# Agent attention with an ELU feed-forward on one core: how the two output accumulators are summed

## The chip, the cores and the metric

The kernel runs on one core of a Trainium2 chip. The metric is the device time of one execution in microseconds; the time before is 998.0 us, the median of three runs (997.5 to 999.86).

## The reference, cut to what matters

```python
def attn(q, k, v, agents):            # q, k, v: 2 x 12480 x 128; agents: 2 x 49 x 128, all fp32
    sm = lambda a, b: softmax(a @ b.T / sqrt(128))
    return sm(q, agents) @ (sm(agents, k) @ v)

def moe(x, w_in, w_out):              # x: 24960 x 128; w_in: 128 x 2048; w_out: 2048 x 128
    h = x @ w_in
    g = where(h > 0, h, exp(min(h, 0)) - 1)
    return g @ w_out                  # 24960 x 128, fp32
```

The product of the agents' values with `w_in` is formed once per batch (a 49 x 2048 matrix A), so that h is the softmax of q over the 49 agents times A.

## The kernel before, in words

**Tiles.** The 24960 tokens are 26 groups of 960, and a group is two halves of 480 columns (T). The 2048 rows of the hidden layer are 8 chunks (NP) of 256, held as two banks of 128 partitions. One **step** s handles one chunk of one half; there are 416 steps. Eight steps in a row (a **cycle**) share one pair of output accumulators, so there are 52 cycles.

**A step** (loop at L720) issues, in this order:
- `p1(s)` (L405): six matmuls on TensorE, in three pairs, write h into a slot of two PSUM banks. There are three slots (`ps_h`, bufs=3). The two matmuls of a pair use different rows of the array and run side by side.
- at the fifth step of each cycle, in a cycle without a "visit" in the step before, `p1(s + 1)` is issued too (L727).
- `p2(s - 4)` (L437): the matmuls with `w_out` add a chunk that is four steps old into the two accumulators: six pairs where g was split into a high and a low part, and otherwise two fp32 products, which the trace shows as four pairs.
- `elu(s)` (L416): ScalarE's Relu of h (L419) and Exp (L422), then VectorE's g (L424), which reads h from PSUM and ends the slot's use.
- `split(s)` (L427): for four or five of eight chunks VectorE casts g (L431), and GpSimd makes the low part in two subtractions (L204).
- extra work from two tables: `mid`, before `elu`, holds the normalisation of the next group's probabilities (`q_mul`, L325) or a subtraction (`e_sub`, L208), always at the fourth step of a cycle; `pre`, at the end of the step, holds score matmuls ("visits", which take an h slot), loads and the rest of the softmax.

There is no scheduler: each engine runs its own instructions in the order in which the loop writes them (`manual_schedule`). Waits come from the tiles: the first matmul into a tile waits until the last reader of the tile that had this place before is done.

**The accumulators** are `o0` and `o1`, one PSUM bank each, in the pool `ps_o` with bufs=1 (L65, L440). So the first `p2` of a cycle, which falls in the fifth step (s % 8 == 4), cannot write before those of the cycle before have been read; and that reading is issued at the end of `p2` in the fourth step (s % 8 == 3).

**The sum** of the two accumulators takes three engines (L454 to L472): VectorE copies `o1` to `ob` (L465, in `p2`); ScalarE copies `o0` to `oa` (L468, between Relu and Exp of the same step's `elu`, through the argument `between`); GpSimd adds `oa` to `ob` (L469); SyncE sends `ob` out (L470). This is done 51 times; the last cycle sums in two pieces on ScalarE and VectorE (L460 to L463).

**The visits** fall on the fourth step of 17 of these 51 cycles (`plan`, L659 to L669, with s % 8 == EDGE == 3). There the score matmuls and one `p1` lie between the last `p2` of a cycle and the first of the next. In the other 34, called quiet here, two `p1` lie there: twelve matmuls in six pairs.

The start-up (about the first 60 us) borrows `o0` and `o1` for scores of k (L537) and for parts of A (L608).

Of the kernel before, what the change touches and what calls it, by code (L numbers as in the profile page):

```python
# [8 lines left out]
F32 = mybir.dt.float32  # L9
# [3 lines left out]
ACTF = mybir.ActivationFunctionType  # L13
ALU = mybir.AluOpType
AX = mybir.AxisListType
# [9 lines left out]
def tile_agent_attention_moe(  # L25
# [10 lines left out]
    nc = tc.nc  # L36
# [7 lines left out]
    T = G // 2  # L44
    NG = N // G
    NR = NG
    S = B * NG * NM
# [17 lines left out]
    ps_o = ctx.enter_context(tc.tile_pool(name="ps_o", bufs=1, space=bass.MemoryType.PSUM))  # L65
# [3 lines left out]
    ident = const.tile([128, 128], F32)  # L69
# [3 lines left out]
    win_sb = big.tile([C, DFF], F32)  # L73
# [63 lines left out]
    def slot(dt=F32):  # L137

        return ps_h.tile([128, 2, 512], dt, tag="h", name="h")
# [9 lines left out]
    def attn_free(ps):  # L149
        if held.pop(id(ps), None) is not None:  # L150
            idle.append(ps)
# [3 lines left out]
    def scores_pe(ps, src, b, lo, hi):  # L155
        for j in range(lo, hi):
            for u in range(0, TP, groups[0]):
                w = min(groups[0], TP - u)
                x = j * TP + u
                nc.tensor.matmul(out=ps[u:u + w, j * NA:(j + 1) * NA], lhsT=src[:, x:x + w], rhs=ag_sb[:, b, :], start=True, stop=True)  # L160
# [3 lines left out]
    def k_copy(ps, r):  # L164
        nc.scalar.activation(out=s_all[:, r, 0:R, :].rearrange("p t a -> p (t a)"), in_=ps[:TP, 0:R * NA], func=ACTF.Copy)

    def k_red(view, r):
        nc.vector.tensor_reduce(out=m_all[:, :, r], in_=view.rearrange("p (t a) -> p a t", a=NA), axis=AX.X, op=ALU.max)  # L168
# [225 lines left out]
    h_t, e_t, g_t, hi_t, lo_t, o_t = {}, {}, {}, {}, {}, {}  # L394

    def at_step(s):

        x, c = divmod(s, NP)
        return x // 2, x % 2, c

    def is_split(s):
        j, half, c = at_step(s)
        return c in SPLITS[half if j * NM + NP + LAG in covered else 0]

    def p1(s):  # L405
        j, half, c = at_step(s)
        h = slot()
        ah, al = A[j // NG, c]
        hi, lo = p_t[j]
        for i, (a, p) in enumerate([(ah, hi), (ah, lo), (al, hi)]):  # L410
            for u, r in enumerate(ROWS):
                x = slice(r, r + NA)
                nc.tensor.matmul(out=h[:, u, 0:T], lhsT=a[x, :], rhs=p[u ^ half][x, :], start=i == 0, stop=i == 2)  # L413
        h_t[s] = h[:, :, 0:T]

    def elu(s, between=None):  # L416

        h, e = h_t.pop(s), x_p.tile([128, 2, T], F32, tag="e", name="e")
        nc.scalar.activation(out=e, in_=h, func=ACTF.Relu, scale=-1.0)  # L419
        if between:  # L420
            between()
        nc.scalar.activation(out=e, in_=e, func=ACTF.Exp, scale=-1.0)  # L422
        g = g_p.tile([128, 2, T], F32, tag="g", name="g", bufs=5)
        nc.vector.scalar_tensor_tensor(out=g, in0=e, scalar=-1.0, in1=h, op0=ALU.add, op1=ALU.max)  # L424
        g_t[s] = g
# [11 lines left out]
    def p2(s):  # L437
        j, half, c = at_step(s)
        if c == 0:
            o_t[0] = ps_o.tile([128, 512], F32, tag="o0", name="o0")  # L440
            o_t[1] = ps_o.tile([128, 512], F32, tag="o1", name="o1")
        g = g_t.pop(s)
        first, last = c == 0, c == NP - 1
        if is_split(s):
            x, hi, lo = SPLIT.index(c), hi_t.pop(s), lo_t.pop(s)
            jobs = [(w[:, x, i], hi[:, i, :]) for w in (w_lo, w_hi) for i in range(2)]
            jobs += [(w_hi[:, x, i], lo[i]) for i in range(2)]
        else:
            jobs = [(w_f[:, PLAIN.index(c), i], g[:, i, :]) for i in range(2)]
        for i, (w, v) in enumerate(jobs):  # L450
            for u, r in enumerate(ROWS):
                x = slice(r, r + 64)
                nc.tensor.matmul(out=o_t[u][:, 0:T], lhsT=w[x], rhs=v[x, :], start=first and i == 0, stop=last and i == len(jobs) - 1)  # L453
        if last:  # L454
            oa = o_p.tile([128, T], F32, tag="oa", name="oa")
            ob = o_p.tile([128, T], F32, tag="ob", name="ob")
            pa, pb = o_t[0], o_t[1]
            n = j * G + half * T
            if s == S - 1:
                for x in (slice(0, T // 2), slice(T // 2, T)):  # L460
                    nc.scalar.activation(out=oa[:, x], in_=pa[:, x], func=ACTF.Copy)
                    nc.vector.tensor_tensor(out=ob[:, x], in0=pb[:, x], in1=oa[:, x], op=ALU.add)
                    nc.sync.dma_start(out=outT[:, n + x.start:n + x.stop], in_=ob[:, x])  # L463
                return None
            nc.vector.tensor_copy(out=ob, in_=pb[:, 0:T])  # L465

            def rest_of_sum():
                nc.scalar.activation(out=oa, in_=pa[:, 0:T], func=ACTF.Copy)  # L468
                nc.gpsimd.tensor_tensor(out=ob, in0=ob, in1=oa, op=ALU.add)  # L469
                nc.sync.dma_start(out=outT[:, n:n + T], in_=ob)  # L470

            return rest_of_sum  # L472

    act, dve, pool = nc.scalar, nc.vector, nc.gpsimd

# [5 lines left out]
    with tc.manual_schedule():  # L481
        with tc.tile_pool(name="pro", bufs=6) as pro:
# [13 lines left out]
            def loads(what):  # L496
                for x in what.split():
                    c, n = x[0], int(x[1:])
                    if c == "k":
                        load_k(0, n, kfrom[n % 9])  # L500
                    elif c == "v":
                        load_v(0, n, vfrom[n])
                    elif c == "q":
                        load_q(n)
                    elif c == "i":
                        win_load(n)
                    elif c == "o":
                        wo_load(n)
                    elif c == "K":
                        load_k(1, n)  # L510
# [3 lines left out]
            nc.sync.dma_start(out=ag_sb, in_=agT)  # L514
            loads("i0 i1 k0 k1 i2 k2 k3 i3 k4 k5")
            two, hk, pair = slot(), slot(), slot()
            ev_ps[0] = two[:, 0, 0:VW]

            def busy(n, cols=512):
                for _ in range(n):  # L520
                    nc.tensor.matmul(out=two[:, 1, 0:cols], lhsT=warm[:, 0:128], rhs=warm[:, 0:cols], start=True, stop=True)
# [12 lines left out]

            def sc(r):
                if r % 2:
                    ps = ps_o.tile([128, 512], F32, tag=f"o{r // 2 % 2}", name=f"o{r // 2 % 2}")  # L537
                else:
                    ps = (pair, hk)[r // 2 % 2][:, 0, :]
                if r:  # L540
                    busy(1, 128)
                scores_pe(ps, k_t.pop((0, r)), 0, 0, R)
                k_red(ps[:TP, 0:R * NA], r)
                k_copy(ps, r)
                attn_free(ps)
# [59 lines left out]
            ev0_out()  # L605
            av_pe()
            av_out()
            o_ps = [ps_o.tile([128, 512], F32, tag=f"o{i}", name=f"o{i}") for i in range(2)]  # L608
            banks = [hk[:, 0, :], o_ps[0], o_ps[1], o_ps[0][:, 256:512]]

            def A_part(c, eng):
                A_pe(0, 512 * c, 512 * c + 512, banks[c])
                A_out(0, 512 * c, 512 * c + 512, eng)
# [7 lines left out]
        o_p = ctx.enter_context(tc.tile_pool(name="o", bufs=1))  # L621
# [70 lines left out]
        for r in range(NR):  # L692
            s0 = visits["e", r]
            x = 75 + NM * (r // 3)
# [23 lines left out]
        at(s0 + 28, A_visit, 1024)  # L718

        for s in range(S + LAG):  # L720
            after = None
            if s < S and s not in h_t and s != NP - LAG - 1:
                p1(s)
            if s == 0:
                A_part(2, dve)
                A_part(3, dve)
            if s % NP == LAG and s > LEAD and s not in covered and s + 1 < S:  # L727
                p1(s + 1)
            if s == 2:
                t = ps_o.tile([128, 512], F32, tag="o1", name="o1")  # L730
                nc.tensor.matmul(out=t[:, 0:T], lhsT=ident, rhs=win_sb[:, 0:T], start=True, stop=True)
            x = s - LAG + (s < LEAD)
            if x >= 0 and s != LEAD:
                after = p2(x)
            if s == NP - LAG - 1:
                p1(s)
            for fn, a in mid.pop(s, []):
                fn(a)
            if s < S:
                elu(s, after)  # L740
                split(s)
            elif after:
                after()
            for fn, a in pre.pop(s, []):
                fn(*a)

# [33 lines left out]
```

## Time and profile before

| what | value |
|---|---|
| median of three runs | 998.0 us (997.5 to 999.86) |
| the profiled execution: its time | 998.71 us |
| the profiled execution: its span, first to last instruction | 995.9 us |
| time around the span | 2.8 us |
| mean granted TensorE clock in the span | 0.996 |
| TensorE matmuls / weight loads, busy share | 98% / 74% |
| VectorE / ScalarE / GpSimd, busy share | 85% / 89% / 69% |

A line of the timeline gives start, duration, engine, line of the code, operation, the tile written and the tiles read, and in brackets how long the engine was idle before and what released it. PE is TensorE's matmuls, PEld its weight loads, DVE VectorE, ACT ScalarE, POOL GpSimd. Ends of matmuls are modelled: a matmul's row is longer than the time until the next one starts, so the pace of TensorE is read from the distance of starts.

### The profile page before, as it was taken

Reading aid. Unit: us, or ns where it says so; the run is one execution under the profiler, and the core shown is the slowest. Engines: PE = TensorE matmul, PEld = TensorE weight load, DVE = VectorE, ACT = ScalarE, POOL = GpSimd, SP = SyncE. Lnnn points to the kernel's source line nnn. Section 1 sums busy time; section 2 is a strip of 40 time slices with the busy share of each in tenths; the row PEclk is TensorE's granted clock in tenths of the full one; section 3 lists DMA queues with packets and bytes.
Section 4 is the critical chain, followed back from the end, with each engine's and each line's share of the span. In section 5 each row is a group of like instructions: output and inputs, shape, how many; then the busy total and the mean of one; then the engine's idle time right before and its main releaser. Section 6 shows DMA issues by size and latency. Waiting matters only on the chain.

```text
span 995.9 us, 25483 instructions
## 1 busy us (share of the span) xinstructions
PE 978.3 (98%) x10380; PEld 734.3 (74%) x10380; DVE 849.7 (85%) x1028; ACT 884.3 (89%) x1017; POOL 687.0 (69%) x559
## 2 busy tenths in 40 slices
PE   7899999999999999999999999999999999999998
PEld 5767777777777777877777777777777777777775
DVE  7778888888888878888888898898888888988887
ACT  4588998988988889998998999989999989989996
POOL 3146666666666766766786886877868867867886
PEclk8999999999999999999999999999999999999999
DMA  9942222223232211101101101011020021001000
GB/s 349 385 148 89 80 72 81 78 74 96 68 85 66 66 41 46 38 31 65 36 23 55 37 26 62 26 56 41 18 76 27 21 66 37 26 12 37 27 20 21
DMA packets 25983, 67.30 MB, mean 68 GB/s; under 512 B 3083, under 2 KB 14963, under 8 KB 25867
## 3 DMA queue, kind: packets, MB, share of 16 engines
q1 hardware_dynamic: 25867, 65.69, 19.5%
q8 instruction: 81, 1.33, 0.6%
q14 instruction: 35, 0.29, 0.1%
HBM read 43.11 MB, written 12.78 MB: 56 GB/s over the span
## 4 chain that ended last, share of the span: by engine, by line
PE 93%; DVE 2%; ACT 2%; DMA 2%; issue 1%; POOL 0%; SPq 0%; DVEq 0%; ACTq 0%
PE o L453 59%; PE h L413 27%; PE h L291 2%; PE h L219 2%; PE h L160 1%; DMA v<-in_vx_dram 1%; PE h L331 1%; DVE g L424 1%; DMA k<-in_kT_dram 1%; ACT e L419 1%; ACT e L422 0%; PE o L160 0%; DVE m_all L168 0%; DVE ex L107 0%; ACT ex L103 0%
## 5 line engine op out<-in xcount | busy, mean ns | idle before, releaser
L204 POOL TENSOR_TENSOR lo<-g,hi 128x480 fp32r<-128x480 f32 x484 | 603.3, 1272 | 253.6 <-DVE hi L431 190.3
L424 DVE SCALAR_TENSOR_TENSOR g<-e,h 128x960 f32<-128x960 f32 x416 | 478.2, 1150 | 109.2 <-ACT e L422 91.7
L419 ACT ACTIVATE e<-h 128x960 f32<-128x960 f32 x416 | 402.5, 967 | 41.0 <-PE h L413 38.5
L422 ACT ACTIVATE e<-e 128x960 f32<-128x960 f32 x416 | 419.1, 1007 | 11.6
L453 PE MATMUL o<-g,w_f 64*128 64x480 f32 x1384 | 307.8, 562 | 0.2 <-DVE g L424 0.2
L413 PE MATMUL h<-py,ahi 49*128 49x480 f32 x832 | 292.4, 431 | 1.4 <-DVE g L424 0.7
L413 PE MATMUL h<-px,ahi 49*128 49x480 f32 x832 | 292.4, 431 | 0.1
L431 DVE CAST hi<-g 128x960 fp32r<-128x960 f32 x243 | 198.4, 816 | 10.8
L453 PEld LDWEIGHTS o<-g,w_f 64*128 64x128 f32 x1384 | 133.2, 185 | 83.1 <-issue 73.6
L413 PEld LDWEIGHTS h<-py,ahi 49*128 49x128 f32 x832 | 149.9, 186 | 39.3 <-issue 23.4
L413 PEld LDWEIGHTS h<-px,ahi 49*128 49x128 f32 x832 | 149.9, 186 | 26.3 <-issue 17.0
L453 PE MATMUL o<-hi,w_lo 64*128 64x480 f32 x972 | 159.4, 403 | 0.0
L413 PE MATMUL h<-px,alo 49*128 49x480 f32 x416 | 157.0, 377 | 0.0
L413 PE MATMUL h<-py,alo 49*128 49x480 f32 x416 | 157.0, 377 | 0.0
L453 PE MATMUL o<-lo,w_hi 64*128 64x480 f32 x972 | 146.9, 378 | 0.0
L453 PE MATMUL o<-hi,w_hi 64*128 64x480 f32 x972 | 146.0, 376 | 0.0
L453 PEld LDWEIGHTS o<-hi,w_lo 64*128 64x128 f32 x972 | 93.4, 186 | 26.0 <-issue 14.3
L453 PEld LDWEIGHTS o<-lo,w_hi 64*128 64x128 f32 x972 | 92.6, 184 | 13.6 <-POOL lo L204 0.3
L453 PEld LDWEIGHTS o<-hi,w_hi 64*128 64x128 f32 x972 | 92.5, 184 | 13.0
L413 PEld LDWEIGHTS h<-py,alo 49*128 49x128 f32 x416 | 76.6, 184 | 5.7
L413 PEld LDWEIGHTS h<-px,alo 49*128 49x128 f32 x416 | 76.6, 184 | 5.6 <-DVE alo L275 0.2
L469 POOL TENSOR_TENSOR ob<-ob,oa 128x480 f32<-128x480 f32 x51 | 70.0, 1372 | 12.2 <-ACT oa L468 12.2
(89 smaller groups left out, 517.7 us busy)
## 6 DMA issues: line engine op xcount, KB each, us to landing
k<-in_kT_dram SPq DMA_DIRECT2D x26, 480.0 KB
q<-in_qT_dram SPq DMA_DIRECT2D x26, 480.0 KB
out_dram<-ob SPq DMA_DIRECT2D x51, 240.0 KB
py<-px SPq DMA_DIRECT2D x104, 91.9 KB
v<-in_vx_dram SPq DMA_DIRECT2D x13, 516.0 KB
v<-in_vx_dram SPq DMA_DIRECT2D x13, 483.8 KB
raw<-in_w_in_dram SPq DMA_DIRECT2D x4, 512.0 KB
raw<-in_w_out_dram SPq DMA_DIRECT2D x4, 512.0 KB
```

Of the source, the lines that this page charges most:

```text
L160: nc.tensor.matmul(out=ps[u:u + w, j * NA:(j + 1) * NA], lhsT=src[:, x:x + w], rhs=ag_sb[:, b, :], start=True, stop=True)
L204: eng.tensor_tensor(out=out, in0=x, in1=hi.bitcast(F32), op=ALU.subtract)
L219: nc.tensor.matmul(out=ps[u:u + 64], lhsT=e[:, j * NA:j * NA + 64], rhs=v_t[b, r][:, j, :], start=(r == rs[0] and j < 2), stop=(r == rs[-1 ...
L291: nc.tensor.matmul(out=ps[u:u + w, t * NA:(t + 1) * NA], lhsT=src[:, x:x + w], rhs=ag_sb[:, j // NG, :], start=True, stop=True)
L331: nc.tensor.transpose(ps[:NA2, u, i * HP:(i + 1) * HP], pp[x, i, 0:NA2], ident[x, x])
L413: nc.tensor.matmul(out=h[:, u, 0:T], lhsT=a[x, :], rhs=p[u ^ half][x, :], start=i == 0, stop=i == 2)
L419: nc.scalar.activation(out=e, in_=h, func=ACTF.Relu, scale=-1.0)
L422: nc.scalar.activation(out=e, in_=e, func=ACTF.Exp, scale=-1.0)
L424: nc.vector.scalar_tensor_tensor(out=g, in0=e, scalar=-1.0, in1=h, op0=ALU.add, op1=ALU.max)
L431: nc.vector.tensor_copy(out=hi_t[s], in_=g_t[s])
L453: nc.tensor.matmul(out=o_t[u][:, 0:T], lhsT=w[x], rhs=v[x, :], start=first and i == 0, stop=last and i == len(jobs) - 1)
L469: nc.gpsimd.tensor_tensor(out=ob, in0=ob, in1=oa, op=ALU.add)
```

## The change

The two accumulators become one tile `o` of two banks. At a cycle's end one VectorE instruction, a `tensor_reduce` with the two banks as the innermost axis, adds them and writes `ob`; the copies on VectorE and ScalarE and the addition on GpSimd go. The output's DMA is issued right behind it. `elu` loses its argument, and it moves ahead of the table `mid`, so that `q_mul` and `e_sub` come between g and the cast. The last cycle's sum keeps its form. In the start-up one tile `outer` of two banks stands in for the borrowed `o0` and `o1`.

```diff
-    def elu(s, between=None):
+    def elu(s):
...
         nc.scalar.activation(out=e, in_=h, func=ACTF.Relu, scale=-1.0)
-        if between:
-            between()
         nc.scalar.activation(out=e, in_=e, func=ACTF.Exp, scale=-1.0)
...
     def p2(s):
         j, half, c = at_step(s)
         if c == 0:
-            o_t[0] = ps_o.tile([128, 512], F32, tag="o0", name="o0")
-            o_t[1] = ps_o.tile([128, 512], F32, tag="o1", name="o1")
+            o_t[0] = ps_o.tile([128, 2, 512], F32, tag="o", name="o")
+        o = o_t[0]
...
-                nc.tensor.matmul(out=o_t[u][:, 0:T], lhsT=w[x], rhs=v[x, :], start=first and i == 0, stop=last and i == len(jobs) - 1)
+                nc.tensor.matmul(out=o[:, u, 0:T], lhsT=w[x], rhs=v[x, :], start=first and i == 0, stop=last and i == len(jobs) - 1)
         if last:
-            oa = o_p.tile([128, T], F32, tag="oa", name="oa")
             ob = o_p.tile([128, T], F32, tag="ob", name="ob")
-            pa, pb = o_t[0], o_t[1]
             n = j * G + half * T
             if s == S - 1:
+                oa = o_p.tile([128, T], F32, tag="oa", name="oa")
+                pa, pb = o[:, 0], o[:, 1]
...
-            nc.vector.tensor_copy(out=ob, in_=pb[:, 0:T])
-
-            def rest_of_sum():
-                nc.scalar.activation(out=oa, in_=pa[:, 0:T], func=ACTF.Copy)
-                nc.gpsimd.tensor_tensor(out=ob, in0=ob, in1=oa, op=ALU.add)
-                nc.sync.dma_start(out=outT[:, n:n + T], in_=ob)
-
-            return rest_of_sum
+            nc.vector.tensor_reduce(out=ob, in_=o[:, :, 0:T].rearrange("p u t -> p t u"), axis=AX.X, op=ALU.add)
+            nc.sync.dma_start(out=outT[:, n:n + T], in_=ob)
...
             two, hk, pair = slot(), slot(), slot()
+            outer = ps_o.tile([128, 2, 512], F32, tag="o", name="o")
...
-                    ps = ps_o.tile([128, 512], F32, tag=f"o{r // 2 % 2}", name=f"o{r // 2 % 2}")
+                    ps = outer[:, r // 2 % 2, :]
...
-            o_ps = [ps_o.tile([128, 512], F32, tag=f"o{i}", name=f"o{i}") for i in range(2)]
-            banks = [hk[:, 0, :], o_ps[0], o_ps[1], o_ps[0][:, 256:512]]
+            banks = [hk[:, 0, :], outer[:, 0, :], outer[:, 1, :], outer[:, 0, 256:512]]
...
             x = s - LAG + (s < LEAD)
             if x >= 0 and s != LEAD:
-                after = p2(x)
+                p2(x)
             if s == NP - LAG - 1:
                 p1(s)
+            if s < S:
+                elu(s)
             for fn, a in mid.pop(s, []):
                 fn(a)
             if s < S:
-                elu(s, after)
                 split(s)
-            elif after:
-                after()
             for fn, a in pre.pop(s, []):
                 fn(*a)
```

## Rows read from the trace of the kernel before

**Rows 1.** The page's first part: busy time of each engine.

```profile
PE 978.3 (98%) x10380; PEld 734.3 (74%) x10380; DVE 849.7 (85%) x1028; ACT 884.3 (89%) x1017; POOL 687.0 (69%) x559
```

**Rows 2.** The page's fourth part: the chain that ended last, by engine.

```profile
PE 93%; DVE 2%; ACT 2%; DMA 2%; issue 1%; POOL 0%; SPq 0%; DVEq 0%; ACTq 0%
```

**Rows 3.** The stages 100 to 300, 300 to 600, 600 to 900 us, summed.

```profile
sum 800.00, PE 799.53 PEld 598.50 DVE 694.29 ACT 733.68 POOL 571.83; mean PE 266.51 PEld 199.50 DVE 231.43 ACT 244.56 POOL 190.61
```

**Rows 4.** Timeline of the end of a quiet cycle, 960.4 to 962.2 us.

```profile
960.40 0.60 PE L453 MATMUL o<-lo,w_hi 64*128 64x480 f32 x4
...
961.03 0.58 ACT L468 ACTIVATE oa<-o 128x480 f32<-128x480 f32 x1 [0.31 <-PE o L453]
961.05 0.38 PE L413 MATMUL h<-px,ahi 49*128 49x480 f32 x1
...
961.07 0.66 DVE L465 COPY ob<-o 128x480 f32<-128x480 f32 x1
...
961.92 0.38 PE L413 MATMUL h<-px,alo 49*128 49x480 f32 x1
...
961.93 0.41 PEld L453 LDWEIGHTS o<-g,w_f 64*128 64x128 f32 x4
...
962.14 0.97 PE L453 MATMUL o<-g,w_f 64*128 64x480 f32 x4
```

**Rows 5.** Timeline of the first quiet cycle's end.

```profile
101.34 0.66 DVE L465 COPY ob<-o 128x480 f32<-128x480 f32 x1
...
102.20 0.42 PEld L453 LDWEIGHTS o<-g,w_f 64*128 64x128 f32 x4
```

**Rows 6.** Groups by line, shapes apart, of VectorE; mean ns follows the busy time.

```profile
L424 DVE SCALAR_TENSOR_TENSOR g<-e,h 128x960 f32<-128x960 f32 x416 | 478.2, 1150 | 109.2 <-ACT e L422 91.7 <-POOL lo L204 6.0 <-PE h L413 3.8
L465 DVE COPY ob<-o 128x480 f32<-128x480 f32 x51 | 33.6, 658 | 2.6
L296 DVE TENSOR_REDUCE mx<-h 124x8 f32<-124x392 f32 x26 | 14.5, 558 | 0.0
L168 DVE TENSOR_REDUCE m_all<-h 120x49 f32<-120x392 f32 x20 | 10.9, 561 | 0.5
L172 DVE TENSOR_REDUCE mrun<-m_all 120x49 f32<-120x637 f32 x1 | 0.8, 814 | 0.0
```

**Rows 7.** Timeline of the one quiet end with a late copy, 214 to 215 us.

```profile
214.10 0.65 DVE L465 COPY ob<-o 128x480 f32<-128x480 f32 x1
...
214.68 0.31 PEld L453 LDWEIGHTS o<-g,w_f 64*128 64x128 f32 x2
```

**Rows 8.** Timeline of a TensorE wait on ScalarE, 84.0 to 85.3 us.

```profile
84.08 0.57 ACT L345 ACTIVATE px<-h 113x480 fp32r<-113x480 f32 x1
...
84.65 0.18 PEld L413 LDWEIGHTS h<-py,ahi 49*128 49x128 f32 x1 [0.75 <-ACT px L345]
...
84.98 0.37 PE L413 MATMUL h<-py,ahi 49*128 49x480 f32 x1
85.01 0.37 PE L413 MATMUL h<-px,ahi 49*128 49x480 f32 x1
```

**Rows 9.** Timeline of a cycle's end with a visit.

```profile
875.10 0.66 DVE L465 COPY ob<-o 128x480 f32<-128x480 f32 x1
...
877.03 0.41 PEld L453 LDWEIGHTS o<-g,w_f 64*128 64x128 f32 x4
```

**Rows 10.** Timeline of a quiet end with the normalisation, 510 to 520 us.

```profile
510.81 0.66 DVE L465 COPY ob<-o 128x480 f32<-128x480 f32 x1
...
511.38 1.18 DVE L325 TENSOR_TENSOR pp<-qe,z 124x392 f32<-124x392 f32 x1
...
513.66 0.66 DVE L431 CAST hi<-g 128x960 fp32r<-128x960 f32 x1
...
514.49 5.17 POOL L204 TENSOR_TENSOR lo<-g,hi 128x480 fp32r<-128x480 f32 x4 [0.86 <-DVE hi L431]
...
518.79 0.41 PEld L453 LDWEIGHTS o<-lo,w_hi 64*128 64x128 f32 x4
```

More of the change, by code (lines that the diff above doesn't have):

```diff
@@ L720, in tile_agent_attention_moe @@
         for s in range(S + LAG):
-            after = None
             if s < S and s not in h_t and s != NP - LAG - 1:
@@ L729, in tile_agent_attention_moe @@
             if s == 2:
-                t = ps_o.tile([128, 512], F32, tag="o1", name="o1")
-                nc.tensor.matmul(out=t[:, 0:T], lhsT=ident, rhs=win_sb[:, 0:T], start=True, stop=True)
+                nc.tensor.matmul(out=outer[:, 1, 0:T], lhsT=ident, rhs=win_sb[:, 0:T], start=True, stop=True)
             x = s - LAG + (s < LEAD)
             if x >= 0 and s != LEAD:
-                after = p2(x)
+                p2(x)
             if s == NP - LAG - 1:
                 p1(s)
+            if s < S:
+                elu(s)
             for fn, a in mid.pop(s, []):
```

## The prediction, made before the changed kernel ran

> **What bounds the kernel now.** I read the busy shares first: matmuls 98%, ScalarE 89%, VectorE 85%, GpSimd 69% [rows 1]. The chain that ended last is 93% TensorE [rows 2]. From 100 to 900 us TensorE is busy 799.53 of 800 us [rows 3]. Since the ends of matmuls are modelled, "busy" could hide waits, so I went to the starts in the timeline. In a quiet cycle's end the pairs start at 961.05 and, four pairs on, at 961.92: 0.217 us apart, and the next pair, the first of the new accumulators, follows 0.22 us later at 962.14 [rows 4]. TensorE goes at its own pace there, right across the place that the change touches. It sets the time of the whole steady part, so work taken off ScalarE or GpSimd is worth nothing in itself, and anything that makes TensorE wait is added to the time, with nothing behind it to win it back.
>
> **The margin at the place of the change.** The last pair into the old accumulators starts at 960.62 (the second of the two pairs in the row of 960.40) and its row ends at 961.00. ScalarE's copy of one bank runs 961.03 to 961.61 and VectorE's of the other 961.07 to 961.73, side by side. TensorE's next load for the same two banks is at 961.93 [rows 4]. So the copy is done 0.20 us before the load. At the first quiet end the distance from copy to load is the same: 101.34 to 102.20, 0.86 us, as 961.07 to 961.93 [rows 5]. That is no chance: the six pairs between are paced by TensorE and the copy starts when TensorE's last pair is done.
>
> **The new instruction.** It reads 960 elements a lane where the copy reads 480. VectorE's reductions take 558 ns for 392 elements and 814 ns for 637, 1.045 ns for one more; 392 elements give 558 ns with 8 results and 561 ns with 49, so results cost next to nothing [rows 6]. For 960: 558 + 568 x 1.045 = 1152 ns. The instruction nearest in size, g, reads 960 elements from two PSUM banks and takes 1150 ns [rows 6]. I take 1.15 us. From below, the copy's 0.66 us is the bound, were only the 480 results to count. From above: no row has two banks taken in turn, element by element; I allow twice the time an element, 0.15 + 2 x 1.0 = 2.15 us. The middle value is nearest to four rows, and the reduction with 49 results already walks its input out of order at no cost.
>
> The Trainium skill (VectorE: DVE Perf Modes, section "The perf-mode tier table") gives `tensor_reduce` no faster mode than one element a cycle, which speaks against the lower bound; by that rule the sum below stays as it is.
>
> **What the wait costs.** How TensorE resumes is seen twice. In the one quiet end whose copy came late, the copy ended at 214.75, and the second of the two loads in the row, which ends at 214.99 and takes 0.18, started at 214.80 or 214.81: 0.05 us behind [rows 7]. Behind a wait on ScalarE (84.08 + 0.57 = 84.65) the load started at 84.65 and the next pair at 84.98; one pace of 0.217 earlier, 84.76, is when the first pair really began, 0.11 us behind the load [rows 8]. So a pair begins 0.16 us after the instruction that it waits for. In the quiet end: reduction from 961.07, ready at 962.22, pair at 962.38 in place of 962.145: 0.235 us lost. The second row half lagged the first by 0.03 us after such a wait (85.01 against 84.98 [rows 8]); it can add that again at the next cycle's end unless a visit evens it out; half of it gives **0.25 us** a quiet end.
>
> The sum over the 51 sums:
> - 33 regular quiet ends: 33 x 0.25 = 8.25 us.
> - The late quiet end, where other work held VectorE until 214.10: 214.10 + 1.15 + 0.16 = 215.41 against 214.80 + 0.11 = 214.91 now [rows 7]: 0.5 us.
> - 17 ends with a visit: copy to load is 1.93 us [rows 9]; 1.15 + 0.05 fits with 0.7 to spare: nothing. At 2.15 us it would miss by 0.3.
>
> That is 8.75 us, less at most 0.2 for a freer ScalarE and GpSimd in the last steps: **8.6 us**.
>
> **What is removed and costs nothing.** ScalarE loses 0.58 us a cycle and the wait of 0.31 before it [rows 4], GpSimd its 51 additions. ScalarE's Exp then starts right behind Relu, and the step's g waits for the end of the reduction and no longer for ScalarE; but TensorE's pace shows no wait for a g [rows 4], so nothing follows. The last cycle's sum is as before. The start-up tile has the same two banks and the same readers: nothing.
>
> **What is moved.** `q_mul` and `e_sub` go behind g and ahead of the cast, at the fourth step. With `q_mul` the order was copy, `q_mul`, g, cast at 513.66; now reduction 510.81 to 511.96, g to 513.13, `q_mul` at its longest 1.18 to 514.31, cast then: 0.65 us later [rows 10]. Behind the cast on VectorE is only the next step's g, and GpSimd's two subtractions wait for it. GpSimd took them up at 514.49 and does each in 1.3; 0.65 later, both are done by 517.8; the load that needs them is at 518.79 [rows 10]. Its cover is a full 1 us, and GpSimd no longer adds `ob` there. The output's DMA now waits on VectorE and not on GpSimd in SyncE's queue, is issued earlier than before and passes no other DMA; `ob` is next written a cycle later. Nothing.
>
> Nothing is done for TensorE: its instructions are the same in number and order. So no gain can pay for the wait.
>
> **Against the forecast, the rules.** TensorE's weight loads are busy 74% [rows 1]. The Trainium skill (Perfetto Trace Analysis, section "Identifying the Most-Contended Engine") says that matmul busy time misleads and that headroom is to be read from the share of weight loads; by that rule a quarter of TensorE's time would be slack, it could take up 0.25 us in 17 and the time would stay at 998. The even starts [rows 4] speak against it: a load of 0.18 us in each pace of 0.217 fills no more than that and still leaves no free pace. The same page (section "Optimizing Scalar/DVE Operations") advises breaking an instruction up where VectorE holds up another engine, the reverse of this change; with the two copies side by side, as now, the sum is zero, with one pass 8.6 us.
>
> **The rivals.**
> - *No wait comes of it* (not slower). The reduction runs at the rate of its results, or TensorE has slack that its rows don't show. It decides where the reduction takes less than 961.93 - 961.07 - 0.05 = 0.81 us; up to nearly 1.0 us the loss stays within 3 us. Time 998.0. For it: the 74% of the loads. Against it: every reduction here is priced by its input. Chance 0.11.
> - *The two banks taken in turn cost double.* Reduction 2.15 us: each quiet end loses 1.25, 34 of them 42 us, the visits up to 0.2 each: about 1042 us. For it: no row shows such a walk. Against it: the strided one is free. Chance 0.05.
> - *The freed engines pay back* (faster). ScalarE's 0.89 us a cycle would be worth up to 45 us, 953, if ScalarE set the pace. Against it are TensorE's even starts, so I give at most 1 us of it at the edges. Chance of over 3 us: 0.03.
> - *The moved work makes the low part late.* It would need 1 us more than I count, in some 25 ends: at most another 10 us, 1017. Chance 0.03.
>
> **How the numbers follow.** The profiled execution took 998.7 us (a span of 995.9 and 2.8 around it), 0.7 above the median. The terms are differences within its span, what lies around is not touched, and I set them on the median: 998.0 + 8.6 = 1006.6 us. The forecast has 0.78. Within it a quiet end can lose 0.15 to 0.36 us (0.05 either way on the reduction, the rest on the resumption): 33 x 0.15 + 0.3 = 5.3 and 33 x 0.36 + 0.7 = 12.6; with a run's scatter of about 1 us the range is 1002.5 to 1012. It leaves out the first three rivals. A difference of 0.3% (3 us) is about what a measurement of this kernel can tell from none. Slower by more: 0.78 + 0.05 + 0.03 = 0.86; within: 0.11; faster: 0.03.
>
> **What the profile after would show.** Right: 51 reductions of 128x480 from 960 at about 1.15 us, starting 0.07 us behind the last pair's row; at each quiet end a load into `o` 0.05 us behind the reduction, and 0.23 to 0.27 us between where the pair starts and where the pace would have put it; none at a visit. Copies and additions gone; ScalarE's busy time down by 51 x 0.58 = 29 us, VectorE's up by 51 x 0.49 = 25. Wrong: an even pace across the quiet ends (no wait), a reduction far from 1.15 us, or TensorE waiting for `lo` or for h.

## The result, and the profile after

The changed kernel took **1006.38 us** (median of four runs, 1005.89 to 1007.26), the kernel before 998.13 in four runs: a ratio of 1.0081, with a 95% interval of 1.0063 to 1.0098. Its profiled execution has a span of 1004.1 us, 8.2 more than before, at a mean clock of 0.998. The forecast was 1006.6 us, with a chance of 0.86 for slower.

The page's busy shares and chain by engine, answering to [rows 1, 2], then the sum of the stages 100 to 900 us, answering to [rows 3]:

```profile
PE 986.2 (98%) x10380; PEld 743.0 (74%) x10380; DVE 861.3 (86%) x1028; ACT 870.6 (87%) x966; POOL 612.2 (61%) x508
...
PE 94%; DVE 3%; ACT 1%; DMA 1%; POOL 1%; issue 1%; SPq 0%; POOLq 0%; DVEq 0%; ACTq 0%
```

```profile
sum 800.00, PE 799.54 PEld 602.64 DVE 697.35 ACT 716.39 POOL 502.86; mean PE 266.51 PEld 200.88 DVE 232.45 ACT 238.80 POOL 167.62
```

By the page GpSimd lost 75 us of busy time and ScalarE 14 (51 copies of 0.573 us went, 29 us, but their rows had overlapped their neighbours'), and the time did not fall for it. TensorE reads as busy for 799.54 of 800 us, as before, although it now waits at every quiet end: modelled ends fill such a wait up. The starts do not. The new instruction by line, and the end of a quiet cycle in the timeline, answering to [rows 4, 6]:

```profile
L463 DVE TENSOR_REDUCE ob<-o 128x480 f32<-128x960 f32 x51 | 59.0, 1158 | 1.6
```

```profile
951.17 0.61 PE L451 MATMUL o<-lo,w_hi 64*128 64x480 f32 x4
...
951.61 0.38 PE L413 MATMUL h<-px,ahi 49*128 49x480 f32 x1
...
951.83 1.16 DVE L463 TENSOR_REDUCE ob<-o 128x480 f32<-128x960 f32 x1
...
952.70 0.38 PE L413 MATMUL h<-px,alo 49*128 49x480 f32 x1
...
953.04 0.30 PEld L451 LDWEIGHTS o<-g,w_f 64*128 64x128 f32 x4 [0.36 <-DVE ob L463]
953.04 1.07 PE L451 MATMUL o<-g,w_f 64*128 64x480 f32 x4
```

The reduction ends at 952.99 and the load follows 0.05 us behind. The pair in the last row is shown at 953.04, but began at about 953.14 by the pairs that follow it (the next starts at 953.55, and two pairs of this fp32 product are 0.40 apart); at the pace of 0.217 it was due at 952.92. So 0.22 us are gone. The late end and an end with a visit, answering to [rows 7, 9]:

```profile
216.08 1.15 DVE L463 TENSOR_REDUCE ob<-o 128x480 f32<-128x960 f32 x1
...
217.28 0.30 PEld L451 LDWEIGHTS o<-g,w_f 64*128 64x128 f32 x4 [0.88 <-DVE ob L463]
```

```profile
881.83 1.16 DVE L463 TENSOR_REDUCE ob<-o 128x480 f32<-128x960 f32 x1
...
883.78 0.41 PEld L451 LDWEIGHTS o<-g,w_f 64*128 64x128 f32 x4
```

At this visit the load comes 0.79 us behind the reduction with no wait. I then took the start of the third pair of each step's `p1` in both traces; how far the changed kernel is behind the kernel before, and at which steps that distance grows or shrinks:

```
step 0: +0.19 us        step 1: +1.69        step 13: +1.42
33 regular quiet ends: +0.19 to +0.25 each, 7.02 together (mean 0.213)
the late quiet end: +0.49      16 of the 17 ends with a visit: 0
steps 168, 184, 231: -0.1 each      step 268: -0.59
step 414: +8.07
```

The first end with a visit does show a wait:

```profile
82.19 1.15 DVE L463 TENSOR_REDUCE ob<-o 128x480 f32<-128x960 f32 x1
...
83.39 0.30 PEld L451 LDWEIGHTS o<-g,w_f 64*128 64x128 f32 x4 [0.22 <-DVE ob L463]
```

The load comes 0.05 us behind the reduction, and the pair behind it is 0.08 us late; TensorE's next wait for ScalarE is shorter by 0.17, so nothing of it is left at step 13. In all, 35 loads wait for the reduction, 34 at quiet ends and this one.

The step of -0.59 is the kernel before's: its profiled execution has a gap at 668 us that nothing in the profile causes and that no later trace has. The 1.5 us between steps 0 and 1 were not forecast. The parts of A in the start-up, changed kernel first, then the kernel before:

```profile
55.34 0.64 PE L257 MATMUL o<-win_sb,avt 128*64 128x256 f32 x4
...
56.54 0.48 DVE L275 SCALAR_TENSOR_TENSOR alo<-o,rz,ahi 113x256 fp32r<-113x256 f32 x1
...
57.17 0.64 PE L257 MATMUL o<-win_sb,avt 128*64 128x256 f32 x4 [1.19 <-DVE alo L275]
```

```profile
55.05 1.08 PE L257 MATMUL o<-win_sb,avt 128*64 128x256 f32 x8
```

Before, the matmuls of the third and fourth quarter ran as one row of eight. Now the fourth quarter's four wait until VectorE has read the third's (57.02), though they write the other bank of `outer`. The trace of the kernel before with the new order alone, which has separate tiles, shows no such step at 1; the other traces that keep both the joint tile and this order of work all lose 1.5 us or more there.

### The profile page after: what moved, and what is told of

Its sections match the earlier page's. It is cut to its first block, busy times and chain, and to the rows that moved or that the text cites. A ratio compares the mean times of both kernels' runs of the same rounds, so it can differ in the third digit from the quotient of the medians.

```text
span 1004.1 us, 25273 instructions
## 1 busy us (share of the span) xinstructions
PE 986.2 (98%) x10380; PEld 743.0 (74%) x10380; DVE 861.3 (86%) x1028; ACT 870.6 (87%) x966; POOL 612.2 (61%) x508
## 4 chain that ended last, share of the span: by engine, by line
PE 94%; DVE 3%; ACT 1%; DMA 1%; POOL 1%; issue 1%; SPq 0%; POOLq 0%; DVEq 0%; ACTq 0%
PE o L451 59%; PE h L413 27%; PE h L219 2%; PE h L291 2%; PE h L160 1%; PE h L331 1%; DVE g L422 1%; DMA k<-in_kT_dram 1%; PE o L160 0%; DVE m_all L168 0%; DVE ex L107 0%; ACT ex L103 0%; PE h L257 0%; ACT s_all L165 0%; POOL lo L204 0%
## 5 line engine op out<-in xcount | busy, mean ns | idle before, releaser
L204 POOL TENSOR_TENSOR lo<-g,hi 128x480 fp32r<-128x480 f32 x484 | 596.7, 1257 | 347.0 <-DVE hi L429 300.0
L451 PE MATMUL o<-g,w_f 64*128 64x480 f32 x1384 | 311.6, 567 | 0.6 <-DVE ob L463 0.5
L429 DVE CAST hi<-g 128x960 fp32r<-128x960 f32 x243 | 200.9, 827 | 9.9
L463 DVE TENSOR_REDUCE ob<-o 128x480 f32<-128x960 f32 x51 | 59.0, 1158 | 1.6
```

The costliest lines, as they stand in the source:

```text
L204: eng.tensor_tensor(out=out, in0=x, in1=hi.bitcast(F32), op=ALU.subtract)
L429: nc.vector.tensor_copy(out=hi_t[s], in_=g_t[s])
L451: nc.tensor.matmul(out=o[:, u, 0:T], lhsT=w[x], rhs=v[x, :], start=first and i == 0, stop=last and i == len(jobs) - 1)
L463: nc.vector.tensor_reduce(out=ob, in_=o[:, :, 0:T].rearrange("p u t -> p t u"), axis=AX.X, op=ALU.add)
```

## The experiments

All ratios are against the kernel before on the same chip. The theory: the time follows from one latency, from the last matmul into the accumulators over the reading of both banks to the next load; what work the reading is, and on which engine, does not matter. Rivals: the reduction's place in VectorE's queue delays g and the low parts; the new order of `elu` and `mid` costs; the three-engine sum would still be better in the new frame.

**One bank read, no sum** (the other accumulator is not read, so the output lacks it).

```diff
-            nc.vector.tensor_reduce(out=ob, in_=o[:, :, 0:T].rearrange("p u t -> p t u"), axis=AX.X, op=ALU.add)
+            nc.vector.tensor_copy(out=ob, in_=o[:, 1, 0:T])
```

> The changed kernel, but VectorE only copies one bank; the other bank is not read and nothing is added, so the output lacks one of the two accumulators. Theory (the number of elements that the one instruction reads decides): 0.66 us, done 0.2 us ahead of the load, no wait, 999.5 us (998.5 to 1000.5). Rival (ScalarE without its copy or the sum's new place in the queues changes the pace): stays over 1003.

Measured: 998.19 us, ratio 1.0007 (0.9997 to 1.0016), a little under the expected range. A quiet end in its timeline:

```profile
944.71 0.66 DVE L463 COPY ob<-o 128x480 f32<-128x480 f32 x1
...
945.59 0.42 PEld L451 LDWEIGHTS o<-g,w_f 64*128 64x128 f32 x4
...
945.80 1.38 PE L451 MATMUL o<-g,w_f 64*128 64x480 f32 x6
```

The load is 0.22 us behind the copy, at TensorE's pace, as in [rows 4]. With the second bank's reading gone, all the quiet ends' loss is gone, with everything else of the change in place. The start-up's 1.5 us stay in this trace (step 1 is 1.64 behind, step 13 still 1.16). The medians differ by 0.3 us only, with an interval up to 1.6, so what the start-up costs is read from the traces' starts and not from the times.

**A reduction of 768 elements** (96 of 480 output columns are not computed; a second DMA sends other data in their place).

```diff
-            nc.vector.tensor_reduce(out=ob, in_=o[:, :, 0:T].rearrange("p u t -> p t u"), axis=AX.X, op=ALU.add)
...
+            m = 384
+            nc.vector.tensor_reduce(out=ob[:, 0:m], in_=o[:, :, 0:m].rearrange("p u t -> p t u"), axis=AX.X, op=ALU.add)
...
```

> The changed kernel with the sum over 384 of the 480 columns only (768 elements; the other 96 columns of the output are not computed, other data is sent in their place by a second DMA). By 1.042 ns an element the instruction takes about 0.96 us and ends about 0.07 us after the time at which the load into o would start by TensorE's pace. Theory (a pair starts 0.16 us behind the end of the instruction, 0.22 behind an undisturbed load, so up to some 0.06 us of lateness costs nothing): lost per quiet end 0.01 to 0.03 us, in all under 1 us beside the start-up's 1.5: 1000 us (999 to 1001.2). Rival (all of the load's lateness, about 0.12 us, is added): 33 x 0.12 = 4 us more, 1003.7.

Measured: 999.25 us, ratio 1.0013 (1.0004 to 1.0021). The group, and one quiet end:

```profile
L464 DVE TENSOR_REDUCE ob<-o 128x384 f32<-128x768 f32 x51 | 48.8, 957 | 1.6
```

```profile
947.12 0.96 DVE L464 TENSOR_REDUCE ob<-o 128x384 f32<-128x768 f32 x1
...
948.13 0.30 PEld L451 LDWEIGHTS o<-g,w_f 64*128 64x128 f32 x4 [0.16 <-DVE ob L464]
```

192 elements (and 96 results) less are 201 ns less, 1.05 ns an element. The load now does wait, and the trace names the reduction, but hardly anything is lost: the load is 0.12 to 0.13 us later against the last pair into the old accumulators than in [rows 4], while the 33 regular quiet ends lose 0.55 us together, 0.017 each. On pace a pair follows its load by 0.22 us (961.93 to 962.14 in [rows 4]), after a wait by 0.11 (953.04 to about 953.14 above), so the first 0.11 us of a load's lateness cost nothing here. A wait that a trace names is not yet a loss. What is left of the 1.1 us over the kernel before is mostly the start-up's: this trace, of an execution 1.1 us above its median, is 2.8 us behind at step 13.

**An unused SBUF copy ahead of the reduction.**

```diff
+            nc.vector.tensor_copy(out=spare, in_=win_sb[:, 0:T])
             nc.vector.tensor_reduce(out=ob, in_=o[:, :, 0:T].rearrange("p u t -> p t u"), axis=AX.X, op=ALU.add)
...
```

> The changed kernel with a copy of 480 elements from SBUF to SBUF on VectorE right ahead of the reduction, whose result is not used; I estimate 0.3 to 0.4 us by the cast's 0.66 for 960. Theory (at a quiet end each 0.1 us by which the reduction ends later is lost whole, at a visit none up to 0.8): 34 x 0.35 = 12 us more, 1018 us (1015 to 1021). Rival (VectorE's load as such sets the pace): 51 x 0.35 = 18 us more, 1024, and as much with the same copy put behind g.

Measured: 1035.32 us, ratio 1.0368 (1.0354 to 1.0383), 29 us above the changed kernel, far over the range. Two ends of its timeline, VectorE, GpSimd and the next load:

```profile
922.55 2.62 POOL L204 TENSOR_TENSOR lo<-g,hi 128x480 fp32r<-128x480 f32 x2 [0.69 <-PE h L413]
923.69 0.40 DVE L463 COPY spare<-win_sb 128x480 f32<-128x480 f32 x1
924.01 1.15 DVE L464 TENSOR_REDUCE ob<-o 128x480 f32<-128x960 f32 x1
...
925.21 0.30 PEld L451 LDWEIGHTS o<-g,w_f 64*128 64x128 f32 x4 [0.53 <-DVE ob L464]
...
939.76 2.41 POOL L204 TENSOR_TENSOR lo<-g,hi 128x480 fp32r<-128x480 f32 x2 [0.95 <-DVE hi L429]
...
941.14 1.30 DVE L463 COPY spare<-win_sb 128x480 f32<-128x480 f32 x1
942.37 1.14 DVE L464 TENSOR_REDUCE ob<-o 128x480 f32<-128x960 f32 x1
...
943.56 0.30 PEld L451 LDWEIGHTS o<-g,w_f 64*128 64x128 f32 x4 [1.48 <-DVE ob L464]
```

The price of the copy was wrong, not the mechanism. I had taken 0.35 us for its delay. It took 0.40 us in 16 of 51 ends, 0.46 to 0.48 in four, and 1.28 to 1.41 in 31, and in each of these 31 it began beside a subtraction of GpSimd's and ended 0.27 us behind that one's end (939.76 + 2.41 = 942.17; 941.14 + 1.30 = 942.44). It was held until GpSimd was done with that one. The Trainium skill (SBUF — State Buffer, section "Who interferes with whom") says that a VectorE copy in a mode that uses two ports and a GpSimd instruction exclude each other for a whole instruction, and that whoever comes first keeps the other out; the 31 ends agree. Behind the delay the loss follows one for one: the load is 0.05 us behind the reduction in both ends above, and TensorE's wait grows from 0.53 to 1.48. Where the copy took 0.40, a regular quiet end loses only 0.10 to 0.23 us more than in the changed kernel, since the copy begins before the last matmul is done; where it was held, 1.08 to 1.23. A copy that was held also uses up the 0.8 us to spare at a visit: 12 visits lose 4.6 us together.

**The same copy behind g of that step.**

```diff
             if s < S:
                 elu(s)
+                if s % NP == EDGE and s > NP:
+                    nc.vector.tensor_copy(out=spare, in_=win_sb[:, 0:T])
...
```

> The changed kernel with the same unused copy of 480 elements on VectorE, 51 times, put behind g of the step that holds the reduction. Theory (only what delays the reduction's end counts; VectorE has room behind g): 1006.4 us (1005.5 to 1007.5). Rival (VectorE's load as such): 1024.

Measured: 1007.10 us, ratio 1.0087 (1.0073 to 1.01), inside the range; the copy took 403 ns in all 51 places, none of them beside GpSimd's work. Work on VectorE costs where it stands between the last matmul and the release of the accumulators, and next to nothing behind g of the same step (0.7 us for 51 copies, against 29 ahead of the reduction). The rival that VectorE's queue makes g and the low parts late falls for this kernel.

**The old order of `elu` and `mid` in the changed kernel.**

```diff
-            if s < S:
-                elu(s)
             for fn, a in mid.pop(s, []):
                 fn(a)
             if s < S:
+                elu(s)
                 split(s)
```

> The changed kernel, but with q_mul and e_sub ahead of elu again. Theory (the place of the normalisation is off the path, since TensorE waits for neither g nor the low part): 1006.4 us (1005.5 to 1007.5), the same 0.21 us at each quiet end. Rival (the order matters: g late behind q_mul, then h slots late): slower than 1008; or the order had cost something: under 1005.

Measured: 1006.10 us, ratio 1.0081 (1.0066 to 1.0096), with the same steps of 0.2 at the quiet ends. In the changed kernel the order is worth nothing.

**The new order alone, in the kernel before.**

```diff
+            if s < S:
+                elu(s, after)
             for fn, a in mid.pop(s, []):
                 fn(a)
             if s < S:
-                elu(s, after)
                 split(s)
```

> The kernel before, with nothing changed but elu put ahead of q_mul and e_sub. Theory (off the path): 998.1 us (997 to 999). Rival (the later cast makes the low part late for TensorE): over 1000. A version that beats the kernel before would be one with more than 3 us less, which the theory excludes: TensorE already goes at its own pace.

Measured: 1003.07 us, ratio 1.0051 (1.0037 to 1.0066): a miss, by 5 us. Against the kernel before this trace falls behind at 23 steps, 4.5 us together, most by 0.17 to 0.20, each at the fourth step behind a `q_mul`; three other steps add 0.6, whose cause is not shown. One of the 23, VectorE and the load that is late:

```profile
515.22 0.66 DVE L465 COPY ob<-o 128x480 f32<-128x480 f32 x1
...
516.75 1.15 DVE L424 SCALAR_TENSOR_TENSOR g<-e,h 128x960 f32<-128x960 f32 x1 [0.88 <-ACT e L422]
...
517.82 0.56 DVE L325 TENSOR_TENSOR pp<-qe,z 124x392 f32<-124x392 f32 x1
518.30 0.65 DVE L431 CAST hi<-g 128x960 fp32r<-128x960 f32 x1
...
518.87 1.14 DVE L424 SCALAR_TENSOR_TENSOR g<-e,h 128x960 f32<-128x960 f32 x1
...
520.78 1.14 DVE L424 SCALAR_TENSOR_TENSOR g<-e,h 128x960 f32<-128x960 f32 x1
...
521.97 0.18 PEld L413 LDWEIGHTS h<-px,ahi 49*128 49x128 f32 x1
```

The last g frees an h slot at 521.92, and `p1`'s load into it follows 0.05 us later. That g begins 5.56 us behind the start of the copy, against 5.35 in the kernel before (its copy at 510.81 in [rows 10]), where the load comes just on time:

```profile
516.16 1.14 DVE L424 SCALAR_TENSOR_TENSOR g<-e,h 128x960 f32<-128x960 f32 x1
```

```profile
517.37 0.19 PEld L413 LDWEIGHTS h<-px,ahi 49*128 49x128 f32 x1
```

There `q_mul` fills the 0.88 us in which VectorE waits for ScalarE's copy and Exp. Put behind g, it leaves that gap empty and pushes the two next g's back. In the changed kernel there is no gap, since ScalarE has no copy to make. The end with the normalisation, answering to [rows 10]:

```profile
514.74 1.16 DVE L463 TENSOR_REDUCE ob<-o 128x480 f32<-128x960 f32 x1
...
515.81 1.14 DVE L422 SCALAR_TENSOR_TENSOR g<-e,h 128x960 f32<-128x960 f32 x1
...
516.87 0.56 DVE L325 TENSOR_TENSOR pp<-qe,z 124x392 f32<-124x392 f32 x1
...
517.35 0.65 DVE L429 CAST hi<-g 128x960 fp32r<-128x960 f32 x1
...
519.84 1.14 DVE L422 SCALAR_TENSOR_TENSOR g<-e,h 128x960 f32<-128x960 f32 x1
```

Here g follows the reduction directly, and the third g begins 5.10 us behind the sum's start, 0.25 sooner than before. So the freed ScalarE does earn something: it pays for the new order. It is not TensorE's new wait at the quiet ends that covers it. The run with one bank has the new order and the 0.66 us copy on VectorE, no copy on ScalarE and no wait at these ends, and it loses nothing at the 23 steps: `p1`'s load there comes 0.57 us or more behind the g that frees its slot (0.27 in one), in the kernel before 0.05 to 0.11, and with the new order alone 0.05 in all 23.

**The three-engine sum in the new frame**, on the joint tile `o`, with the new order.

```diff
-            nc.vector.tensor_reduce(out=ob, in_=o[:, :, 0:T].rearrange("p u t -> p t u"), axis=AX.X, op=ALU.add)
+            pa = o[:, 0, 0:T]
+            nc.vector.tensor_copy(out=ob, in_=o[:, 1, 0:T])
+
+            def rest_of_sum():
+                nc.scalar.activation(out=oa, in_=pa, func=ACTF.Copy)
+                nc.gpsimd.tensor_tensor(out=ob, in0=ob, in1=oa, op=ALU.add)
...
```

> The changed kernel, but with the sum by three engines again (VectorE copies one bank, ScalarE the other between Relu and Exp, GpSimd adds), still on the joint tile and with elu ahead of the normalisation. Theory (the length of the one VectorE instruction makes TensorE wait at the 34 quiet ends, about 0.21 us each, 7 us in all, and the joint tile of the start-up costs another 1.2 to 1.5 us): the load into o is again 0.20 us behind the copy, no wait at any quiet end but the late one, time 999.5 us (998.5 to 1000.5). Rival (the new order or the joint tile makes the wait): time stays at 1005 to 1007.

Measured: 1028.32 us, ratio 1.0319 (1.0293 to 1.0344): a miss by 29 us. From its waits by line, and an end in its timeline:

```profile
ACT oa L470 <- DVE ob L467: 52.7, 51, 1.6
```

```profile
990.12 0.66 DVE L467 COPY ob<-o 128x480 f32<-128x480 f32 x1
990.81 0.57 ACT L470 ACTIVATE oa<-o 128x480 f32<-128x480 f32 x1 [1.01 <-DVE ob L467]
991.27 0.99 ACT L422 ACTIVATE e<-e 128x960 f32<-128x960 f32 x1
...
992.37 1.16 DVE L424 SCALAR_TENSOR_TENSOR g<-e,h 128x960 f32<-128x960 f32 x1 [1.60 <-ACT e L422]
```

ScalarE's copy waits for VectorE's each of the 51 times, though they read different banks: side by side in [rows 4], one after the other here. Against the run with the new order alone, the joint tiles (this one and the start-up's) are the only difference, and the time is 25 us longer. The accumulators are free at 991.38, 0.60 us behind VectorE's copy, Exp and g come late, and behind g the h slots: TensorE's share of the chain falls from 93% to 61%, ScalarE's rises to 20%. The joint tile is itself a cost for whoever uses its banks separately.

**The start-up: the last quarter in another tile.**

```diff
-            banks = [hk[:, 0, :], outer[:, 0, :], outer[:, 1, :], outer[:, 0, 256:512]]
+            banks = [hk[:, 0, :], outer[:, 0, :], outer[:, 1, :], pair[:, 1, :]]
```

> The changed kernel with the last quarter of A in the start-up written to a bank of the tile pair in place of a part of outer. In the trace of the changed kernel that quarter's matmuls start at 57.17, 0.14 us behind VectorE's last read of the third quarter in the other bank of the same tile; before, they ran together with the third quarter's at 55.05. Theory (the joint tile makes them wait there, and the start-up loses 1.2 to 1.5 us by it): first sum of a cycle about 1.2 to 1.5 us earlier than in the changed kernel, 1005.1 us (1004 to 1006). Rival (the start-up's difference is that of two executions' DMA and clock): no difference, 1006.4.

Measured: 1005.95 us, ratio 1.0075 (1.0061 to 1.0088), at the edge of the expected range and 0.45 from the rival's 1006.4: inconclusive by time. The trace says why. Step 1 is now only 0.5 us behind (0.4 of it from step 0), but step 2 falls back by 1.07: its `p1` takes the slot of `pair`, and waits for that quarter's reading. The wait moved one step on:

```profile
57.67 0.48 DVE L275 SCALAR_TENSOR_TENSOR alo<-h,rz,ahi 113x256 fp32r<-113x256 f32 x1
...
58.31 0.46 PE L413 MATMUL h<-px,ahi 49*128 49x480 f32 x1 [0.83 <-DVE alo L275]
```

**The start-up: both quarters' matmuls first, then their reading.**

```diff
-                A_part(2, dve)
-                A_part(3, dve)
+                for c in (2, 3):
+                    A_pe(0, 512 * c, 512 * c + 512, banks[c])
+                for c in (2, 3):
+                    A_out(0, 512 * c, 512 * c + 512, dve)
```

> The changed kernel with the matmuls of the last two quarters of A issued together, ahead of the reading of either; nothing else. Theory: the 1.5 us that the changed kernel is late from step 1 on come from this one place, where the last quarter's matmuls wait for VectorE to read the other bank of the joint tile. Issued first, they wait for nothing, and only the two quarters' reading on VectorE lies behind them, as before the change: step 1 at 0.2 to 0.5 us behind the kernel before, step 13 likewise, and the whole at 1005.1 (1004.5 to 1005.8) with the quiet ends as they are. Rival: the delay has another cause (ScalarE's reading of the first two quarters, the first use of the accumulators at step 4) or is taken up later: step 13 stays 1.2 to 1.6 behind and the time at 1006.4. A second rival: the wait only moves on to the next slot, as it did with the quarter in another tile: step 2 late by 1 us, 1006.

Measured: 1005.41 us, ratio 1.0072 (1.0058 to 1.0085), within the expected range; 0.97 us under the changed kernel, with overlapping intervals. The trace decides:

```profile
54.65 1.07 PE L257 MATMUL o<-win_sb,avt 128*64 128x256 f32 x8
...
57.20 0.48 DVE L275 SCALAR_TENSOR_TENSOR alo<-o,rz,ahi 113x256 fp32r<-113x256 f32 x1
...
57.73 1.07 PE L723 MATMUL o<-win_sb,ident 128*128 128x480 f32 x2 [0.52 <-DVE alo L275]
```

The eight matmuls stand in one row again, and step 1 loses 0.10 us against step 0 in place of 1.50. Of the 1.40 saved, 0.44 are lost again at step 3, where a matmul into one bank of `outer` still waits for the reading of the other (the second rival, a step later and at under half its size). At step 13 it is 0.42 behind, counted from step 0, and the changed kernel 1.23. The quiet ends are as they were. This is the best that was found for the changed kernel; no version was found that beats the kernel before, where TensorE already keeps its own pace at these ends.

## Why the prediction was right, and where it was not

- **The bound and the mechanism**: right. TensorE at its own pace, a reduction that makes the accumulators late, nothing to win it back. Reading one bank gives the loss back, 768 elements do all but 0.55 us, and a delay of the reduction is paid in full at the quiet ends.
- **The reduction**: forecast 1.15 us, measured 1.158. The two banks in turn cost 6 ns more than the 1152 worked out from the other reductions; the rival of twice the price is out.
- **The resumption**: forecast 0.05 to the load and 0.11 on to the pair; both came as said: 0.05 at each of the 34 quiet ends, and about 0.11 in the end shown.
- **A quiet end**: forecast 0.25, measured 0.213 on average, 7.02 us in place of 8.25 for the 33. The lag of the second row half, counted with 0.015, did not show: the reduction starts 0.42 us behind the last pair's start, where the copy started 0.45 behind [rows 4]. That is the 0.235 without the lag, less 0.03, plus 0.008 for the reduction.
- **The late end**: 0.5 forecast, 0.49 measured. **The visits**: nothing in the sum, as forecast, but the 0.7 us to spare did not hold at all of them. In one, with a lighter visit, the load came only 0.10 us behind the reduction; at the first the load waited, and the 0.08 us that this cost were covered by a later wait for ScalarE.
- **"The start-up tile has the same two banks and the same readers: nothing"**: this step failed. It cost 1.5 us at step 1 and 1.23 by step 13. I compared banks and readers and left out that one tile makes a write to one bank wait for a read of the other. The run with both quarters' matmuls first gets 0.8 of the 1.23 back by order alone.
- **"What is moved"**: nothing followed, as said, but I weighed the wrong cover. I asked whether the low part would be late; in the kernel before the order alone costs 5 us through the h slots that g frees. And I took the cast 0.65 us later; it came 0.24 sooner (2.61 us behind the sum's start, 2.85 in [rows 10]), since g starts sooner and `q_mul` took 0.56 in place of 1.18. The cost was covered by what I had called worthless, the freed ScalarE.
- **The busy times**: forecast 29 us less for ScalarE and 25 more for VectorE, by the page 14 less and 12 more. ScalarE's copies had overlapped their neighbours' rows (in [rows 4] the copy ends at 961.61 and Exp began at 961.50). On VectorE the reductions did add 25, but the `q_mul` fell from 22.6 to 15.6 us together and the `e_sub` from 15.5 to 13.6. The time does not hang on either.
- **The sum**: 7.02 + 0.49 + 1.23 + 0.19 at step 0, less 0.3 and 0.59, is 8.04 us; forecast 8.6. The 0.59 is a gap in one execution of the kernel before and no effect of the change; without it the sum is 8.63, while the medians differ by 8.25. That the forecast is so near is in part luck: the quiet ends were set 1.23 us too high, and the start-up was missed by 1.23.
- **The rivals**: a rate by results is out: 480 results took 1158 ns, where the copy's 480 took 658. That TensorE's weight loads at 74% mean slack is out as well: the Trainium skill's rule on headroom (Perfetto Trace Analysis, section "Identifying the Most-Contended Engine") would have kept the time, and here the share stayed at 74% while the time rose by 0.8%.

## What to carry to other kernels

Where TensorE keeps its own pace, price the release of a PSUM accumulator as a latency, from the last matmul to the next load; total work saved on other engines does not count against it, and two copies side by side release sooner than one pass over both banks. Putting two banks into one tile ties their users together in the program's waits: look for every writer and reader that used them apart, in the start-up too. Look for waits in the distances of matmul starts against the pace, not in TensorE's busy share, which read 799.5 of 800 us with and without them.

## What was not expected of the hardware

- An fp32 copy within SBUF on VectorE takes 0.40 us alone and up to 1.41 beside GpSimd's subtractions, ending 0.27 us behind the one that holds it (31 of 51 places, and four more where it began 0.2 us before that one's end). It holds GpSimd as well. In eight of the 16 places where it took 0.40 no GpSimd instruction ran beside it; in the other eight it began just before the end of a subtraction, and the next subtraction took 1.39 to 1.47 us in place of 1.23.
- A load that a reduction held up, 0.12 us later than at TensorE's pace, cost its pair 0.017 us on average, in a trace that shows the load waiting.
